# Twenty-eight dummy products behind a chunk's state products, and the first r·k moved behind the table of k

## The chip, the cores and the metric

The kernel runs on one core of one Trainium2 chip. The metric is device time in microseconds, as the median of several executions. Profiles are of one execution each, with the times of all instructions counted from the first.

## What is computed

Three stages follow each other on batches of 4 x 768 tokens with 8 heads of 48 channels (384 channels in all). The dense products of the MLP are each done as three products of a high and a low part.

```
# 1. linear attention with a decaying state, per batch and head
for t in range(S):
    y[t]  = r[t] @ (state + outer(u * k[t], v[t]))
    state = w[:, None] * state + outer(k[t], v[t])
# 2. a gated MLP with a mix over tokens
h = gelu(x @ w_in);  u, v = split(h)
v_n = layernorm(v) * g_ln
v_s = einsum('ts,bsd->btd', w_sg, v_n) + b_sg[None, :, None]
x2  = x + (u * v_s) @ w_out
# 3. a gated projection with a causal convolution of 5 taps
out = (sigmoid(conv5(x2)) * (x2 @ w_val)) @ w_out2
```

## The kernel before, in words

**Attention.** The 768 tokens of a batch are six chunks of 128, so there are 24 chunks, numbered 0 to 23 ("chunk 8" is the ninth). A chunk's loads are `rp`, `kp` and `v`. TensorE transposes r and the scaled k (`att_T`, line 652), which are multiplied by tables of powers of w on the way out of PSUM (`tabR`, `tabK`; made in `tables`, lines 321 to 357). Then come scores (`S_products`, line 678; from chunk 6 on `S_blocks`, line 749), the state's products k^T v (`KV_products`, line 705; from chunk 6 on `KV_blocks`, line 783) and the outputs (lines 840 to 875). GpSimd makes r·k (`dv`), which for chunk 0 stands in `tables` as `dv0`. The results go through HBM into the rows `xf`.

**MLP.** For each batch: projections V0 to V5 (the half v of h, 128 tokens each, `mlp_V`) and U00 to U13 (the half u, 384 tokens by 128 channels, `mlp_U`), then the mix over tokens (`mlp_SG`, S00 to S13, with `wsg`, the parts of w_sg, and `vh`, the normalised v), `mlp_O1`, `mlp_VAL` and `mlp_O2`. Each product of the three parts is a call of `three` (lines 1091 to 1093). w_sg is scaled by a power of two that its own sum of squares sets: ScalarE squares it (line 444), TensorE adds (line 465), VectorE makes the scale (lines 473 to 479), ScalarE and VectorE make the parts (`psg`, line 494 and a helper), and SP turns them with transposing DMAs (line 497).

**What sets the order.** All of the program's order is fixed when it is built. `go` is a planner: it has streams of TensorE's work (attention and MLP), and chains of steps on ScalarE (A), VectorE (V), GpSimd (P) and SP's queue (Q), with assumed costs, and puts out instructions in the order of planned times. On the chip each engine goes through its list in order and waits on semaphores. The first lines of the lists are written by hand (`consts`, `load_w`, `tables`).

**Dummy products.** `fill(n)` issues n products of a matrix of ones with itself, 128 columns each, into the PSUM tile `warm` (`self.pf`), whose result nobody reads. The planner calls it in the gaps that it sees for TensorE in the first 30 us of its plan; `S_products` and `att_Y` call it by hand for chunk 0.

**PSUM.** Its eight banks are three pools: one bank for `pw`, NPA = 4 for attention (`pa`) and 7 - NPA = 3 for the MLP (`pm`). `warm` is the first tile of `pm`. A bank goes to another tile when the last instruction on the tile that has it has been issued, and that tile's first product then waits until it is done with; the planner itself counts three tokens for `pm`.

```
"pa": NPA, "pm": 7 - NPA
self.pf = self.pm.tile([P, 512], F32, tag="pm", name="warm")
nc.tensor.matmul(self.pf[:, 0:P], self.onesb, self.onesb, start=True, stop=True)
```

**Places that matter below.** The small vectors g_ln and b_sg are loaded by `load_small`, whose place in SP's queue is set by `AFTER_SM`. At the end of the last batch `mlp_O2` puts `LAST_FILL` dummies behind the last products.

Of the kernel before, what the change touches and what calls it, by code (L numbers as in the profile page):

```python
# [32 lines left out]
class Kern:  # L33
# [145 lines left out]
    def go(self, streams, choose):  # L179
# [3 lines left out]
        while True:  # L183
# [9 lines left out]
            if n is None:  # L193
# [5 lines left out]
                t = min(soon)  # L199
                n = int((t - self.now) * (FILL0 if self.now < 14000 else FILL) / (112 if self.now < 4000 else 56)) if self.now < FILL_END else 0  # L200
                if n:
                    self.fill(FILLS.get(self.n_fill, n))
                    self.n_fill += 1
# [116 lines left out]
    def tables(self):  # L320

        nc = self.nc
        M = Q
        self.tabR = self.const([HR, NP, P], F32, "tabR")
        self.tabK = self.const([HR, NP, P], F32, "tabK")
        self.W = self.const([HR, NP], F32, "W")
        q = self.Rst(F32)[:HR, 0:NP * (Q + 1)].rearrange("d (p n) -> d p n", p=NP)
        wq, rw = (self.const([HR, NP], F32, n) for n in ("wq", "rw"))
        t = self.Rst(F32)[:HR]
        z, y, e = (t[:, n * NP * M:(n + 1) * NP * M].rearrange("d (p n) -> d p n", n=M) for n in range(3))  # L330
        nc.gpsimd.memset(z, 0.0)
        nc.gpsimd.memset(q[:, :, 0:1], 1.0)


        nc.vector.tensor_scalar(wq, self.wP, W_LEAST, W_MOST, ALU.max, ALU.min)

        def scan(src, dst):
            for p in range(NP):
                nc.vector.tensor_tensor_scan(dst[:, p], src[:, p:p + 1].to_broadcast([HR, M]), z[:, p], 1.0, ALU.mult, ALU.add)

        scan(wq, q[:, :, 1:])
        nc.scalar.copy(self.tabR[:, :, 0:M], q[:, :, 0:M])
        nc.gpsimd.tensor_mul(self.tabR[:, :, M:], q[:, :, 0:M], q[:, :, M:].to_broadcast([HR, NP, M]))
        nc.vector.reciprocal(rw, wq)
        scan(rw, y)


        nc.vector.scalar_tensor_tensor(e, q[:, :, 1:], -1.0, y, ALU.mult, ALU.mult)
        nc.vector.scalar_tensor_tensor(self.tabK[:, :, 0:M], e, 2.0, y, ALU.add, ALU.mult)

        def second(e):
            e.tensor_mul(self.tabK[:, :, M:], self.tabK[:, :, 0:M], self.tabK[:, :, M - 1:M].to_broadcast([HR, NP, M]))
            e.tensor_mul(self.W, q[:, :, M:].rearrange("d p o -> d (p o)"), q[:, :, M:].rearrange("d p o -> d (p o)"))

        self.dv0(nc.gpsimd)
        second(nc.gpsimd)
        self.mark("tabS0", T_S)

# [313 lines left out]
    def S_products(self, i):  # L672
        nc = self.nc
        rT, kT = self.kr[i]
        pA, pB = self.ps_a(), self.ps_a()
        for p in range(NP):
            for ps, r0 in ((pA, 0), (pB, 64)):
                nc.tensor.matmul(ps[:, p * P:(p + 1) * P], kT[r0:r0 + D, p, :], rT[r0:r0 + D, p, :], start=True, stop=True)
        self.mark(("S", i))
        if not i:  # L680
            self.fill(12)
        mb = self.mask.unsqueeze(1).to_broadcast([P, NP, P])
        parts = self.scores[i] = []
        for n, ps in enumerate((pA, pB)):

            def masked(e, ps=ps):
                t = self.wp.tile([P, NP, P], F32, tag="sc", name=self.nm("sc"), bufs=2)
                e.tensor_mul(t, ps.rearrange("s (p t) -> s p t", t=P), mb)
                parts.append(t)

            self.chain(("sc", i, n), ("V", 602.0, masked, ["sc"], ["pa"]), after=[("Y", i - 1)] if i else [], prio=pr(i))
# [80 lines left out]
    def KV_blocks(self, i, X):  # L772

        nc = self.nc
        c = i % NCH
        kS, vt = self.kS[i], self.vt[i]
        halves = range(2 if c != NCH - 1 else 1)
        c0 = NP * Q
        for p in range(NP):
            for j in range(2):  # L780
                for h in halves:
                    ts = slice(h * Q, (h + 1) * Q)
                    nc.tensor.matmul(X[h][64 * j:64 * j + 64, c0 + p * D:c0 + (p + 1) * D], kS[ts, 2 * p + j, :], vt[ts, 2 * p + j, :], start=True, stop=True)  # L783
        self.mark(("KV", i))
        for h in halves:
            n = 2 * i + h
            kv = X[h][:HR, c0:c0 + NP * D].rearrange("d (p e) -> d p e", e=D)
            given = []
            fresh = not c and not h

            def add(e, h=h, n=n, kv=kv, given=given, fresh=fresh):
                told, tnew = self.T2[n % 3], self.T2[(n + 1) % 3][:, :, 0:D]
                e.tensor_copy(tnew, kv) if fresh else e.tensor_add(tnew, kv, told[:, :, 0:D])  # L793
                self.X_read(i, h, given)

            def decay(e, n=n):
                tnew = self.T2[(n + 1) % 3][:, :, 0:D]
                if e is nc.scalar:
                    for p in range(NP):
                        e.activation(tnew[:, p], tnew[:, p], AF.Copy, scale=self.W[:, p:p + 1])  # L800
                else:
                    e.tensor_mul(tnew, tnew, self.W.unsqueeze(2).to_broadcast([HR, NP, D]))

            self.chain(
                ("kv", i, h), ("V", 290.0, add, [], given), *([("AP", {"A": 1120.0, "P": 560.0}, decay)] if h else []),
                after=[("Y", i - 1)] + (["T2"] if i == QUAD else []) + ([("kv", i, 0)] if h else [("kv", i - 1, 1)] if c else []), prio=pr(i),
            )
# [444 lines left out]
    def mlp_O2(self, b, half, q, dst=None):  # L1252
# [13 lines left out]
        if b == B - 1 and half:  # L1266
            if q == 2:
                pz = self.ps_m()
                for _ in range(LAST_FILL):
                    nc.tensor.matmul(pz[:, 0:P], self.onesb, self.onesb, start=True, stop=True)  # L1270
# [182 lines left out]
def pr(i):  # L1453

    return 0 if i < NCH else PR_A if i >= 2 * NCH or i < FROM_B else PR_B
# [6 lines left out]
FROM_B, PR_B = 9, 2.5  # L1462
RAW, PR_RAW = 13, 2.5
QUAD, PAST_NS = 6, 520
AFTER_SG, AFTER_SM, AFTER_CW = 6, 6, 9
WA, WM = 4, 4
NW = 3
NR, NS, NA, NX, NY, NL, NV, NPA = 12, 10, 3, 3, 2, 3, 2, 4
# [9 lines left out]
HOLD_G, HOLD_S, TURN = 200.0, 0.0, 1500.0  # L1478
HOLD = {"gelu": HOLD_G, "sigmoid": HOLD_S}
FILL, FILL0 = 0.6, 0.8  # L1480
FILL_END = 30000.0
FIRST = "V0 U00 V1 U01 V2 U02 V3 U03 V4 V5"
LAST = "U10 S00 U11 S01 U12 S02 U13 S03 O00 O01 O02 S10 S11 A00 A01 A02 S12 S13 P00 O10 P01 O11 P02 O12 A10 A11 A12 P10 P11 P12"
# [1 line left out]
BODY = "U10 S00 U11 S01 U12 S02 U13 S03 O00 O01 O02 S10 S11 A00 A01 A02 S12 S13 P00 O10 P01 O11 P02 O12 v0 A10 u00 A11 v1 A12 v2 u01 u02 v3 u03 P10 v4 P11 P12 v5"  # L1485
END = "U10 S00 U11 S01 U12 S02 U13 S03 O00 O01 S10 S11 O02 S12 S13 A00 A01 A02 O10 O11 O12 P00 P01 A10 A11 A12 P02 P10 P11 P12"
LATER = ['a', 'a', 'a', 'a', 'a', 'a']
FILLS = {}
LAST_FILL = 5
W_LEAST, W_MOST = 0.75, 1.0  # L1490
N_OK = HR * NP

# [41 lines left out]
```

## Time and profile before

| | us |
|---|---|
| median of 3 runs | 434.7 (433.62 to 434.74) |
| the profiled execution's own time | 432.49 |
| its span, first to last instruction | 430.7 |
| TensorE products busy | 411.3 (96%) |
| VectorE busy | 346.6 (80%) |
| ScalarE busy | 207.1 (48%) |
| GpSimd busy | 208.9 (49%) |
| mean granted TensorE clock | 0.996 |

A row of the profile's order of time has a start and a duration in us, the engine, the line, the operation, the tiles as out<-in, a count if rows were joined, and in brackets the idle time of the engine just before, with what ended it. The ends of products are modelled: of products that follow each other the distance of the starts is what one costs. [...]

### The profile page before, as it was taken

The page shows a single profiled execution, that of the slowest core. Times are in us where ns is not written, and L with a number is a line of the kernel's source. Part 1 is how long each engine was busy: PE and PEld are TensorE (multiplying, and loading weights), DVE is VectorE, ACT ScalarE, POOL GpSimd, SP SyncE. Part 2 cuts the span into 40 slices and gives each one's busy share as a digit, 9 for nine tenths or more (in the row PEclk, how much of TensorE's full clock was granted, in tenths as well). Part 3 has the DMA queues.
Part 4 walks back from the last instruction along what each step waited for, and adds up shares of the span by engine and source line. Part 5 has one row for each costly group of instructions (what it writes and reads, how often), then busy time and mean ns, then how long its engine had stood idle before and what let it go on. Part 6 is the DMA issues. An engine that isn't in the chain of part 4 may idle for free. (4 is left out here: it accounts for less than half of the span.)

```text
span 430.7 us, 11575 instructions
## 1 busy us (share of the span) xinstructions
PE 411.3 (96%) x4616; PEld 346.9 (81%) x4616; DVE 346.6 (80%) x740; ACT 207.1 (48%) x439; POOL 208.9 (49%) x243
## 2 busy tenths in 40 slices
PE   7988998889999999999999999899999999999996
PEld 7776787857787999877887999777878989776896
DVE  6887899987899788788989799777786696649992
ACT  2546667754464486534253486532132763104152
POOL 6776976466267657673597757652110322100000
PEclk9999999989999999999999999999999999999999
DMA  6998997699646716764558541632002001000012
GB/s 164 204 237 190 256 274 188 129 198 204 171 87 133 195 47 152 175 163 107 126 124 211 148 113 37 176 84 55 20 2 91 18 2 55 2 0 2 0 38 79
DMA packets 128955, 50.15 MB, mean 116 GB/s; under 512 B 90752, under 2 KB 126720, under 8 KB 128896
## 3 DMA queue, kind: packets, MB, share of 16 engines
q1 hardware_dynamic: 128464, 48.76, 46.5%
q8 instruction: 38, 0.62, 0.6%
q10 hardware_dynamic: 432, 0.59, 0.4%
q14 instruction: 21, 0.17, 0.1%
HBM read 37.54 MB, written 9.44 MB: 109 GB/s over the span
## 5 line engine op out<-in xcount | busy, mean ns | idle before, releaser
L1091 PE MATMUL pm<-wsg,vh 128*128 128x384 f16 x192 | 63.6, 331 | 0.6 <-DVE S L1242 0.6
L1093 PE MATMUL pm<-wsg,vh 128*128 128x384 f16 x192 | 63.2, 329 | 0.0
L1092 PE MATMUL pm<-wsg,vh 128*128 128x384 f16 x192 | 63.1, 329 | 0.0
L1212 DVE SCALAR_TENSOR_TENSOR words<-xf,cw,words 128x384 f32<-128x384 f32 x72 | 44.3, 615 | 3.3 <-ACT words L1210 2.3
L1424 POOL TENSOR_TENSOR R<-S,R 128x384 fp32r<-128x384 f32 x16 | 16.0, 1008 | 56.3 <-ACT R L1450 51.2
L1424 POOL TENSOR_TENSOR ks<-kp,tabS 128x384 f32<-128x384 f32 x24 | 24.3, 1012 | 26.8 <-PE pa L783 13.4
L1091 PE MATMUL pm<-R,win 128*128 128x384 f32 x96 | 34.1, 355 | 1.0 <-ACT S L1148 1.0
L1091 PE MATMUL pm<-R,wout 128*128 128x384 f32 x96 | 33.2, 346 | 0.0
L1092 PE MATMUL pm<-R,wout 128*128 128x384 f32 x96 | 32.3, 336 | 0.1
L1093 PE MATMUL pm<-R,win 128*128 128x384 f32 x96 | 32.3, 337 | 0.0
L1092 PE MATMUL pm<-R,win 128*128 128x384 f32 x96 | 32.2, 335 | 0.0
L1093 PE MATMUL pm<-R,wout 128*128 128x384 f32 x96 | 32.2, 335 | 0.0
L1178 DVE SCALAR_TENSOR_TENSOR S<-pm,gs,b_bc 128x384 f32<-128x384 f32 x32 | 19.6, 614 | 15.2 <-PE pm L1093 13.9
L1450 ACT CAST R<-S 128x384 fp32r<-128x384 f32 x33 | 16.7, 511 | 29.3 <-DVE S L1424 14.4
L1091 PEld LDWEIGHTS <-vh 128*128 128x128 f16 x192 | 19.0, 99 | 14.5 <-issue 3.5
L1093 PE MATMUL pm<-win,R 128*128 128x512 f32 x72 | 28.7, 398 | 1.7 <-DVE R L988 1.7
L1424 POOL TENSOR_TENSOR R<-xf,R 128x384 fp32r<-128x384 f32 x12 | 12.1, 1012 | 37.0 <-ACT R L1450 21.3
L1091 PE MATMUL pm<-win,R 128*128 128x512 f32 x72 | 28.7, 398 | 0.5 <-ACT R L984 0.5
L1093 PEld LDWEIGHTS <-vh 128*128 128x128 f16 x192 | 18.9, 98 | 12.6 <-issue 0.3
L1092 PEld LDWEIGHTS <-vh 128*128 128x128 f16 x192 | 19.0, 99 | 12.0 <-issue 1.5
L1092 PE MATMUL pm<-win,R 128*128 128x512 f32 x72 | 28.4, 395 | 0.0
L1424 POOL TENSOR_TENSOR rs<-rs,exps 128x1 f32<-128x1 f32 x24 | 14.3, 597 | 29.0 <-DVE rs L1114 20.1
(196 smaller groups left out, 1226.6 us busy)
## 6 DMA issues: line engine op xcount, KB each, us to landing
rp<-in_r_dram SPq DMA_DIRECT2D x24, 192.0 KB, 3.6
kp<-in_k_dram SPq DMA_DIRECT2D x24, 192.0 KB, 4.0
v<-in_v_dram SPq DMA_DIRECT2D x24, 192.0 KB, 3.8
xd<-yT SPq DMA_DIRECT2D x48, 96.0 KB, 2.2
xf<-xd SPq DMA_DIRECT2D x24, 192.0 KB, 2.7
raw<-in_r_dram SPq DMA_DIRECT2D x43, 96.0 KB, 2.6
raw<-in_k_dram SPq DMA_DIRECT2D x43, 96.0 KB, 2.5
out_dram<-S SPq DMA_DIRECT2D x21, 192.0 KB, 1.9
```

What stands on the lines that cost most here:

```text
L1091: nc.tensor.matmul(ps, lh, rh, start=m == 0, stop=False)
L1092: nc.tensor.matmul(ps, lh, rl, start=False, stop=False)
L1093: nc.tensor.matmul(ps, ll, rh, start=False, stop=m == total - 1)
L1178: ("V", 529.0, lambda e: e.scalar_tensor_tensor(t, pg[:, :TH], self.gs[:, d:d + 1], self.b_bc[:, ts], ALU.mult, ALU.add), [], ["pm"]),
L1212: eng.scalar_tensor_tensor(t, row[:, j:j + TH], self.cw[:, e, j:j + 1], t, ALU.mult, ALU.add)
L1424: self.made.append(call(*a, **kw))
L1450: return "AV", {"A": 413.0, "V": 269.0}, lambda e: e.copy(dst, src()) if hasattr(e, "copy") else e.tensor_copy(dst, src()), [], list(give)
```

## The change

Four things move. (1) Behind the state products of chunk 8 stand 28 dummies. (2) In `tables` the product r·k of chunk 0 moves from ahead of `tabK`'s second half to behind it, on GpSimd. (3) The numbers of dummies change: behind the first scores 22 for 12, in the planner's gaps ahead of them 14 for 29 and 9 for 14 (the later gaps keep their counts), and 16 for 5 at the very end. (4) `load_small` follows chunk 5's loads, not chunk 6's.

```diff
         def second(e):
             e.tensor_mul(self.tabK[:, :, M:], ...)
+            self.dv0(e)
             e.tensor_mul(self.W, ...)
-        self.dv0(nc.gpsimd)
         second(nc.gpsimd)
...
         if not i:
-            self.fill(12)
+            self.fill(22)
...
                     nc.tensor.matmul(X[h][64 * j:64 * j + 64, ...], kS[ts, 2 * p + j, :], vt[ts, 2 * p + j, :], start=True, stop=True)
+        self.fill(KV_FILL.get(i, 0))
         self.mark(("KV", i))
...
-AFTER_SG, AFTER_SM, AFTER_CW = 6, 6, 9
+AFTER_SG, AFTER_SM, AFTER_CW = 6, 5, 9
...
+KV_FILL = {8:28}
...
-FILLS = {}
-LAST_FILL = 5
+FILLS = {7:8,8:2,9:3,10:1,13:3}
+LAST_FILL = 16
```

**TensorE, the first projections.** The rows are the end of U01 and the beginning of V2 (third of the v projections), with the semaphores that a product waits for. Before:

```order
L1091 MATMUL pm_1025<-R_607,win_96 128x384
L1092 MATMUL pm_1025<-R_607,win_96 128x384
L1093 MATMUL pm_1025<-R_607,win_97 128x384
L1091 MATMUL pm_1043<-win_96,R_605 128x512
L1092 MATMUL pm_1043<-win_97,R_605 128x512
```

The same place of the changed program:

```order
L1092 MATMUL pm_1015<-R_597,win_96 128x384
L1093 MATMUL pm_1015<-R_597,win_96 128x384
L1094 MATMUL pm_1015<-R_597,win_97 128x384
L1092 MATMUL pm_1033<-win_96,R_595 128x512 [waits Activation_49]
L1093 MATMUL pm_1033<-win_97,R_595 128x512
```

No product has moved, but V2's first product now waits for ScalarE: `warm` is in use until chunk 8, so the projections ahead of it go round two banks, and V2 takes the one that U00 had.

**GpSimd, the tables.** The rows follow `tabR`'s second half. Before:

```order
L343 TENSOR_TENSOR tabR<-Rst_156 112x4x64
L589 TENSOR_TENSOR dv_136<-rp_123,kp_126 128x8x48
L352 TENSOR_TENSOR tabK<-tabK 112x4x64
L353 TENSOR_TENSOR W<-Rst_156 112x4
L1424 TENSOR_TENSOR dv_136<-dv_136,u_bc 128x8x48
```

Of the changed program:

```order
L343 TENSOR_TENSOR tabR<-Rst_156 112x4x64
L352 TENSOR_TENSOR tabK<-tabK 112x4x64
L589 TENSOR_TENSOR dv_136<-rp_123,kp_126 128x8x48
L354 TENSOR_TENSOR W<-Rst_156 112x4
L1425 TENSOR_TENSOR dv_136<-dv_136,u_bc 128x8x48
```

The product r·k has gone past one instruction, and stands ahead of the small product W.

**SP, the small loads.** Before:

```order
L910 DMA xf_519<-xd_59 128x3x128
L530 DMA rp_124<-in_r_dram 128x8x48
L530 DMA kp_127<-in_k_dram 128x8x48
L316 DMA g<-in_moe_g_ln_dram 128x4x1
L318 DMA b_bc<-in_moe_b_sg_dram 128x768
```

Of the changed program:

```order
L911 DMA xf_509<-xd_59 128x3x128
L316 DMA g<-in_moe_g_ln_dram 128x4x1
L318 DMA b_bc<-in_moe_b_sg_dram 128x768
L530 DMA rp_124<-in_r_dram 128x8x48
L530 DMA kp_127<-in_k_dram 128x8x48
```

The two small loads have gone past the loads of r and k of chunk 7.

## Rows read from the trace of the kernel before

**Rows 1.** Window of 2 us: busy us (instructions) of each engine, granted clock, DMA.

```profile
90.00:92.00 2.00, 2.00 (x8) 0.97 (x8) 1.69 (x2) 2.00 (x3) 1.51 (x2) 0.50 1.26 262
```

**Rows 2.** Order of time, TensorE and VectorE from chunk 8 to the mix over tokens.

```profile
88.07 0.43 DVE L757 COPY_PREDICATED dv<-mask,pa 128x256 f32<-128x256 int16 x1
...
88.60 0.62 PE L652 MATMUL pa<-ident,rp 128*112 128x128 f32 x4 [2.09 <-issue]
...
89.61 0.52 PE L1091 MATMUL pm<-wsg,vh 128*128 128x384 f16 x1
...
92.53 0.45 PE L1091 MATMUL pm<-wsg,vh 128*128 128x384 f16 x1
...
93.14 0.33 PE L1091 MATMUL pm<-wsg,vh 128*128 128x384 f16 x1
...
93.31 0.33 PE L1092 MATMUL pm<-wsg,vh 128*128 128x384 f16 x1
```

**Rows 3.** Order of time, the projections U00, V2 and U02 and ScalarE's gelu.

```profile
54.89 0.44 PE L1091 MATMUL pm<-R,win 128*128 128x384 f32 x1
...
58.12 0.39 PE L1091 MATMUL pm<-win,R 128*128 128x512 f32 x1
...
60.36 0.85 ACT L1148 ACTIVATE S<-pm 128x384 f32<-128x384 f32 x2
...
60.88 0.44 PE L1091 MATMUL pm<-R,win 128*128 128x384 f32 x1 [0.51 <-ACT S L1148]
```

**Rows 4.** Order of time, chunk 7's state products and VectorE's reading of them.

```profile
71.03 0.63 PE L783 MATMUL pa<-v,ks 64*64 64x48 f32 x32
...
72.51 0.35 DVE L793 TENSOR_TENSOR T<-pa,T 112x192 f32<-112x192 f32 x1
```

**Rows 5.** Order of time, projections U12 and U13, ScalarE, and chunk 8's scores.

```profile
77.66 2.59 ACT L494 ACTIVATE psg<-st,sb 128x768 f16<-128x768 f32 x3 [0.49 <-DVE sb L478]
...
78.45 0.33 PE L1091 MATMUL pm<-R,win 128*128 128x384 f32 x1
...
80.15 1.23 ACT L1148 ACTIVATE S<-pm 128x384 f32<-128x384 f32 x3
...
80.67 0.45 PE L1091 MATMUL pm<-R,win 128*128 128x384 f32 x1 [0.49 <-ACT S L1148]
...
85.36 0.69 PE L749 MATMUL pa<-rT,kT 48*64 48x64 f32 x32 [0.85 <-DVE vh L1424]
```

**Rows 6.** Order of time, TensorE, the next mix over tokens.

```profile
129.09 0.32 PE L1091 MATMUL pm<-wsg,vh 128*128 128x384 f16 x1 [0.60 <-DVE S L1242]
```

**Rows 7.** Line 339, the scans of both tables: count, ns min/median/max, start us.

```profile
L339 DVE TENSOR_TENSOR_SCAN Rst<-wq,Rst x4: 266/268/295, 4.3 to 4.8; 112x64 f32<-112x64 f32 x4
L339 DVE TENSOR_TENSOR_SCAN Rst<-rw,Rst x4: 259/464/1047, 5.2 to 6.9; 112x64 f32<-112x64 f32 x4
```

**Rows 8.** Order of time, the head.

```profile
5.86 1.01 POOL L589 TENSOR_TENSOR dv<-rp,kp 128x384 f32<-128x384 f32 x1
...
8.86 0.60 PE L366 MATMUL pa<-ident,tabK 112*128 112x112 f32 x4 [1.55 <-POOL tabK L352]
...
10.45 0.51 ACT L379 ACTIVATE words<-Rst 128x384 f32<-128x384 f32 x1 [0.47 <-DMA Rst<-in_moe_w_in_dram]
...
11.64 1.00 POOL L1424 TENSOR_TENSOR ks<-kp,tabS 128x384 f32<-128x384 f32 x1 [1.28 <-DVE words L1424]
...
11.85 0.84 PE L222 MATMUL warm<-onesb 128*128 128x128 bf16 x12
```

**Rows 9.** Order of time, SP's small loads, and GpSimd's r·k of chunk 7.

```profile
37.39 3.05 SPq L316 DMA_DIRECT2D g<-in_moe_g_ln_dram  x1
...
40.49 0.50 SPq L318 DMA_DIRECT2D b_bc<-in_moe_b_sg_dram  x1
...
48.52 1.02 POOL L1424 TENSOR_TENSOR kp<-rp,kp 128x384 f32<-128x384 f32 x1
```

**Rows 10.** Order of time, TensorE, the dummies at the very end.

```profile
426.46 0.45 PE L1270 MATMUL pm<-onesb 128*128 128x128 bf16 x5
```

## The prediction, made before the run

> **What bounds the kernel now.** I read the page first: TensorE's products cover 96% of the span, so I looked for the stretches where it waits, and for those where it is slow. [...] From 93.14 on its products follow each other every 0.17 us; the ten between 89.61 and 92.53, counted along the order of time, take nine steps in 2.92 us [rows 2]. The projections before that are not TensorE's alone: U02 idled 0.51 us and U13 0.49 us for ScalarE's gelu, chunk 8's scores 0.85 us for other engines [rows 3, 5]. So up to 90 us TensorE, ScalarE and VectorE wait for each other in turn. Later TensorE waits little, but where it does, as for 0.60 us at 129.09, it is for VectorE [rows 6]. What a stretch before 90 us loses is passed on; what TensorE alone gains near 90 us may be lost at the next wait for VectorE.
>
> **The 28 dummies, their own time.** Twelve dummies of the head take 0.84 us, so one costs at most 0.07 us [rows 8], and 28 at most 1.96 us. They stand where TensorE idles 2.09 us [rows 2]: cost 0. The cover is the wait for VectorE's copy; were it gone, the cost would be up to 1.96 us.
>
> [...]
>
> **What they cost elsewhere: a PSUM bank.** The dummies write `warm`, the first tile of the MLP's pool of three banks. Before, its last use lay ahead of the first projection. Now it lies behind chunk 8, so V0 to U13 share two banks, as the new wait of V2's first product shows. Step by step:
>
> - V2 takes U00's bank. Before, it started at 58.12, in a third bank. U00's gelu is the first of the pair at 60.36, and U02, which waited for just that, started at 60.88 [rows 3]. So V2 starts at 60.88, 2.76 us late. U02's idle 0.51 us is then gone, and it starts 60.88 - 58.12 - 0.51 = 2.25 us late. I carry 2.2.
> - Behind U02 TensorE has no wait until chunk 7's state products at 71.03, so these end at 73.9, not 71.66. VectorE read them at 72.51 [rows 4], so VectorE is late by 1.4 (73.9 - 72.51) to 2.2 us. The scale of w_sg and then `psg` on ScalarE hang on it: 77.66 becomes 79.1 to 79.9 [rows 5]. I take 1.6 us, nearer the lower end, since `psg` itself follows an idle 0.49 us of ScalarE that may take up some.
> - ScalarE's gelu of U10 stands behind `psg` in its queue: 80.15 becomes 81.75. U12 needs the bank of U10, so it starts at the end of that gelu, 81.75 + 1.23/3 = 82.2, not at 78.45 [rows 5]. U13, nine steps of 0.17 behind, starts at 83.7, not 80.67: 3.0 us late.
> - The idle 0.85 us ahead of chunk 8's scores swallows a part [rows 5]: 2.2 us late. The state products, the dummies, VectorE's copy and the start of the mix follow, so it starts at 89.61 + 2.2 = 91.8.
>
> **What is left at the end.** TensorE makes good 1.4 of 2.2 us. VectorE, which is not faster, stays late by what it was: between 1.4 (its lateness at chunk 7) and 2.2 (at chunk 8). At 129.09 TensorE waits for VectorE, so from there the lateness of VectorE counts. I take 1.9 us, nearer the later end.
>
> [...]
>
> **The head.** The third scan of `tabK` takes 1.047 us, where the same scan for `tabR` takes 0.268 [rows 7], and it stands beside GpSimd's r·k, 5.86 to 6.87 [rows 8]. With r·k behind the table, `tabK` can be 0.78 us earlier, its transposes start at 8.1 and not 8.86, and the first scores come earlier too. But behind them ScalarE waits for w_in's DMA until 10.45, VectorE for that, and GpSimd's scaled k at 11.64 for VectorE [rows 8]; none of it depends on `tabK`. So the gain is 0 (bounds: 0 and 0.8). The moved r·k runs from about 8.1 to 9.1, and GpSimd's idle 1.28 us ahead of the scaled k takes it up. Of the dummies, 22 behind the scores take at most 22 x 0.07 = 1.54 us. With the scores ending 0.78 us earlier, at 11.1, they are done by 12.6, ahead of the scaled k at 12.64: cost 0, or up to 0.7 us if the scores don't move.
>
> **The small loads.** The load of r and k of chunk 7 is issued 3.05 + 0.50 = 3.55 us later, and SP is back in step behind it. Its first reader on GpSimd starts at 48.52 [rows 9], so a load that goes out at 40 has over 8 us: cost 0, and at most the same 3.55 us if that reader waited. The 16 dummies at the end, at most 0.09 us each, are done by 427.9 [rows 10], inside the span of 430.7: cost 0.
>
> **Sum.** 0 + 1.9 + 0 = +1.9 us on the profiled execution's own 432.49, so 434.4. The median of the runs is 434.7, 2.2 us above that execution, so the forecast is **436.6**. About 0.3% (1.3 us) is what a measurement of this kernel can tell from no change.
>
> **Rivals.**
>
> *The clock falls in the new gaps* (slower by more). TensorE now idles 2.76 us ahead of V2 and, by the steps above, some 2 us ahead of U12. The clock fell behind a gap of 2.09 us [rows 1, 2], so it may fall there. It costs about what the old fall cost, 1.4 us, and that delays the gelu that others wait for. The time is 436.6 + 1.4 = 438.0. Against it: TensorE works at full clock on both sides of these gaps, and the idle 1.55 us ahead of `tabK`'s transposes passed without a fall [rows 8]. [...]
>
> *Faster: the lateness never reaches chunk 8.* The mechanism is that chunk 8's scores are set by other engines, as their idle 0.85 us suggests. It decides at TensorE being under 0.85 us late there. Then only the clock counts: 434.7 - 1.4 = 433.3. For it: the wait named in the row. Against: U12 must wait for a gelu that stands behind `psg`, which alone makes U13 over 1.5 us late even with `psg` in time.
>
> *Nothing left at the end.* The clock's 1.4 us meets a lateness that VectorE's waits have worn down to its lower bound, 1.4 us: 434.7 - 1.4 + 1.4 = 434.7, or up to 436.0 where TensorE keeps only part of the gain.
>
> *The change does not hold the clock*: the fall has other causes than this gap. Then 1.4 us of TensorE's gain is missing; by the sum VectorE sets the end anyway, with 2.2 us late at most plus what is lost in the mix: 437 to 438, in one case with the first rival.
>
> **How the numbers follow.** The forecast, with its own range of 436.1 to 437.3 (VectorE late by 1.4 to 2.6), has 0.42. The first and last rival together have 0.18, faster 0.18, nothing left 0.22. So slower by over 0.3% has 0.42 + 0.18 = 0.60, within 0.3% 0.22, faster 0.18. The range reaches down to the faster case, 433.2, and up to the clock's case with 0.6 us for the bounds of the head, 438.6.
>
> **What would show it.** Right: V2 starts right behind U00's gelu, over 2 us idle ahead of it; U12 starts behind U10's gelu; the mix over tokens starts at 91 to 92.5 with products every 0.17 us; the clock is 1.00 from 86 to 96; at 129 the same product starts 1.4 to 2.6 us later. In the head the third scan is near 0.27 us, and the scaled k is still at 11.6. Wrong: V2 at 58, or the mix at 89.6 or before. A granted clock of 0.50 between 58 and 66 would be the first rival.

## The result, and the profile after

The changed kernel takes 438.28 us (median of 6 runs, 437.18 to 441.07), the kernel before 433.89 us in the same comparison (6 runs). The ratio is 1.0105, with a 95% interval of 1.0075 to 1.0134: the change makes the kernel 1% slower. The profiled execution took 440.0 us, with a span of 438.2 us; that of before took 432.49 and 430.7. The two stand at opposite ends of their kernels' executions (the change's second highest of six; before's below all but one of its six), so of the 7.5 us between these two spans only 4.4 us are the difference of the medians.

The order of time shows the steps of the prediction (start, duration, engine, line, operation; in brackets the idle time before and what ended it). The row at 61.78 is V2, the row at 84.69 is U12, those at 95.77 and 97.24 are the first and the tenth product of the mix:

```profile
55.88 0.44 PE L1092 MATMUL pm<-R,win 128*128 128x384 f32 x1
...
61.26 0.85 ACT L1149 ACTIVATE S<-pm 128x384 f32<-128x384 f32 x2
61.78 0.80 PE L1092 MATMUL pm<-win,R 128*128 128x512 f32 x1 [2.50 <-ACT S L1149]
...
65.57 0.60 ACT L1130 ACTIVATE A<-pm 128x512 f32<-128x512 f32 x1 [3.04 <-PE pm L1094]
66.20 0.69 DVE L1131 BATCH_NORM_STATS2 bst<-A 128x6 f32<-128x512 f32 x1 [3.81 <-ACT A L1130]
...
81.68 2.59 ACT L494 ACTIVATE psg<-st,sb 128x768 f16<-128x768 f32 x3 [0.49 <-DVE sb L478]
...
84.69 0.44 PE L1092 MATMUL pm<-R,win 128*128 128x384 f32 x1 [1.79 <-ACT S L1149]
...
91.44 0.67 PE L749 MATMUL pa<-rT,kT 48*64 48x64 f32 x32
...
92.50 1.74 PE L222 MATMUL warm<-onesb 128*128 128x128 bf16 x28
94.88 0.62 PE L652 MATMUL pa<-ident,rp 128*112 128x128 f32 x4 [0.65 <-issue]
95.77 0.33 PE L1092 MATMUL pm<-wsg,vh 128*128 128x384 f16 x1
...
97.24 0.33 PE L1092 MATMUL pm<-wsg,vh 128*128 128x384 f16 x1
...
134.84 0.32 PE L1092 MATMUL pm<-wsg,vh 128*128 128x384 f16 x1 [0.55 <-DVE S L1243]
...
431.82 1.07 PE L1271 MATMUL pm<-onesb 128*128 128x128 bf16 x16
```

Against the rows of before, the same instruction starts this much later: U00 0.99 us (55.88 against 54.89), V2 3.66 (against 58.12), both in [rows 3]; `psg` 4.02 and U12 6.24 and chunk 8's scores 6.08 [rows 5]; the mix 6.16, its tenth product 4.71 [rows 2]; the product that waits for VectorE 5.75 [rows 6]; the dummies of the end 5.36 [rows 10]. Between the mix's first and tenth product TensorE makes good 1.45 us: the clock is held there, at 1.00 from 94 to 98 us, where before it was 0.50 in 90 to 92 [rows 1]. The span itself is 7.5 us longer, so 2.1 us come behind the last product.

The windows of 2 us (busy us of each engine, granted clock as a share of full speed, DMA) show where the clock fell instead:

```profile
62.00:64.00 2.00, 2.00 (x5) 1.60 (x6) 0.39 (x1) 0.53 (x2) 1.47 (x2) 0.50 0.91 271
...
86.00:88.00 2.00, 2.00 (x8) 2.00 (x7) 1.94 (x5) 0.49 (x1) 0.81 (x2) 0.50 1.12 91
...
92.00:94.00 2.00, 2.00 (x67) 1.95 (x60) 1.41 (x4) 1.50 (x4) 1.03 (x2) 1.00 0.60 119
```

Ahead of both falls TensorE idled for a gelu, 2.50 us before V2 and 1.79 us before U12: one long idle ahead of each fall. In this execution the clock was also at 0.50 in 45 to 47 us, behind an idle 1.17 us that ended at 42.45. There the change was still 0.58 us ahead of before (43.03); with the fall, U00 is 0.99 us late. The row of the same place before shows no fall behind an idle 1.07 us, nor does the change with 5 dummies at the end behind 1.18 us, so this idle alone does not make the fall.

The head (the first row is the third scan of `tabK`), and the output's DMA at the end (the last row is of all outputs from 415 us on, issue to landing; the 4.0 is the last output's):

```profile
5.95 0.26 DVE L339 TENSOR_TENSOR_SCAN Rst<-rw,Rst 112x64 f32<-112x64 f32 x1
...
8.06 0.61 PE L366 MATMUL pa<-ident,tabK 112*128 112x112 f32 x4 [0.24 <-POOL tabK L352]
...
10.82 0.52 ACT L379 ACTIVATE words<-Rst 128x384 f32<-128x384 f32 x1 [1.64 <-DMA Rst<-in_moe_w_in_dram]
...
12.02 0.99 POOL L1425 TENSOR_TENSOR ks<-kp,tabS 128x384 f32<-128x384 f32 x1 [1.43 <-DVE words L1425]
...
432.52 0.34 ACTq L1272 DMA_DIRECT2D out_dram<-S  x1
...
DMA to landing us min/median/max: 1.8/2.0/4.0
```

The third scan took 1.05 us before and now takes 0.26, and `tabK` is 0.80 us earlier. Nothing comes of it, because ScalarE waits for w_in's DMA [rows 8]. The last issue ends at 432.86, 5.3 us ahead of the end of the span. Before, the rows at the same places read:

```profile
5.96 1.05 DVE L339 TENSOR_TENSOR_SCAN Rst<-rw,Rst 112x64 f32<-112x64 f32 x1
...
427.16 0.34 ACTq L1271 DMA_DIRECT2D out_dram<-S  x1
...
DMA to landing us min/median/max: 1.9/1.9/2.8
```

There it is 3.2 us (430.7 less 427.50); the 2.8 is the output before the last, and the last one's landing is in no row.

### The profile page after: what moved, and what is told of

Its sections match the earlier page's. It is cut to its first block, busy times and chain, and to the rows that moved or that the text cites. A ratio compares the mean times of both kernels' runs of the same rounds, so it can differ in the third digit from the quotient of the medians.

```text
span 438.2 us, 11636 instructions
## 1 busy us (share of the span) xinstructions
PE 417.9 (95%) x4645; PEld 353.4 (81%) x4645; DVE 345.1 (79%) x740; ACT 206.8 (47%) x439; POOL 208.7 (48%) x243
## 5 line engine op out<-in xcount | busy, mean ns | idle before, releaser
L1092 PE MATMUL pm<-R,win 128*128 128x384 f32 x96 | 34.8, 363 | 1.8 <-ACT S L1149 1.8
L1094 PE MATMUL pm<-R,win 128*128 128x384 f32 x96 | 32.9, 343 | 0.0
L1093 PE MATMUL pm<-R,win 128*128 128x384 f32 x96 | 32.9, 343 | 0.0
L1092 PE MATMUL pm<-win,R 128*128 128x512 f32 x72 | 29.5, 410 | 2.9 <-ACT S L1149 2.5
L1094 PE MATMUL pm<-win,R 128*128 128x512 f32 x72 | 29.2, 405 | 1.8 <-DVE R L989 1.8
L1092 PEld LDWEIGHTS <-vh 128*128 128x128 f16 x192 | 18.7, 98 | 14.2 <-issue 3.0
L1093 PE MATMUL pm<-win,R 128*128 128x512 f32 x72 | 28.9, 401 | 0.0
L1094 PEld LDWEIGHTS <-vh 128*128 128x128 f16 x192 | 18.8, 98 | 12.4
L1149 ACT ACTIVATE S<-pm 128x384 f32<-128x384 f32 x32 | 15.4, 486 | 27.4 <-PE pm L1094 27.4
```

Of the source, the lines that this page charges most:

```text
L1092: nc.tensor.matmul(ps, lh, rh, start=m == 0, stop=False)
L1093: nc.tensor.matmul(ps, lh, rl, start=False, stop=False)
L1094: nc.tensor.matmul(ps, ll, rh, start=False, stop=m == total - 1)
L1149: self.chain(("u", b, half, f), ("A", ("gelu", 371.0), lambda e: e.activation(t, pu[:, :TH], AF.Gelu_apprx_tanh), [], ["pm"]))
```

## The experiments

All times are medians; each kernel ran beside the kernel before on one chip, and the ratio is to that. The kernel before itself took 433.9 to 435.2 us in the five comparisons, so an expected time can be missed by a microsecond for that reason alone; the ratios decide. In the traces of all runs but the one with xf ahead of a transpose, the engines do the same work in the same order as in the kernel that the run starts from, apart from the dummies.

| kernel | us | before, same comparison | ratio (95%) |
|---|---|---|---|
| the change | 438.28 | 433.89 | 1.0105 (1.0075 to 1.0134) |
| 28 dummies in their own bank | 435.85 | 434.32 | 1.0024 (0.9990 to 1.0057) |
| before + 28 dummies on `warm` | 436.65 | 434.32 | 1.0045 (1.0010 to 1.0081) |
| before + 1 dummy on `warm` | 437.64 | 434.32 | 1.0084 (1.0056 to 1.0113) |
| the change without the 28 | 435.00 | 434.32 | 1.0016 (0.9987 to 1.0045) |
| before + 16 dummies at the end | 437.21 | 435.22 | 1.0050 (1.0021 to 1.0079) |
| the change, 5 at the end | 439.49 | 435.22 | 1.0084 (1.0053 to 1.0116) |
| before + 28 in their own bank | 435.24 | 435.22 | 1.0010 (0.9981 to 1.0039) |
| the change, own bank, 5 at the end | 434.90 | 435.22 | 0.9992 (0.9968 to 1.0016) |
| the change, its new gaps filled | 438.80 | 434.52 | 1.0089 (1.0055 to 1.0123) |
| before + own bank + dummies ahead of `okb` | 434.39 | 434.52 | 0.9995 (0.9970 to 1.0020) |
| the same, xf ahead of a transpose | 447.89 | 434.52 | 1.0286 (1.0245 to 1.0327) |
| before + own bank + `okb`, none at the end | 434.03 | 435.12 | 0.9977 (0.9950 to 1.0003) |

**The bank: dummies in a tile of their own.**

```diff
-        self.fill(KV_FILL.get(i, 0))
+        n_kv = KV_FILL.get(i, 0)
+        if n_kv:
+            own = self.ps_m()
+            for _ in range(n_kv):
+                nc.tensor.matmul(own[:, 0:P], self.onesb, self.onesb, start=True, stop=True)
```

Expected:

> The changed kernel, but the 28 dummies write a pm tile of their own, taken at chunk 8, so warm is released after the head again. Theory (the bank): V2 starts again at 58 to 59 us with no wait for a gelu, U12 with none, the new falls of the clock at 61 and 85 us are gone, the mix over tokens starts at 89.5 to 90.5 us at full clock; the time is 432.5 to 434.5, 4 to 5.5 us under the changed kernel. Rival (the dummies' own time, or the other edits): nothing but the tile has changed, so the time stays at 437 to 439.

Measured: 435.85 us, a ratio of 1.0024, between the two expected ranges: 1.35 us above the top of the first. Against the change's 1.0105 this is 0.8% or 3.5 us less, and the two intervals do not meet. Its order of time has the old starts again:

```profile
58.12 0.39 PE L1096 MATMUL pm<-win,R 128*128 128x512 f32 x1
...
60.78 0.45 PE L1096 MATMUL pm<-R,win 128*128 128x384 f32 x1 [0.42 <-ACT S L1153]
...
89.36 0.33 PE L1096 MATMUL pm<-wsg,vh 128*128 128x384 f16 x1
...
100.10 5.32 SPq L497 DMA_TRANSPOSE wsg<-psg  x3
...
106.15 0.38 SPq L956 DMA_DIRECT2D xf<-xd  x1
...
110.00 0.36 DVE L1429 CAST R<-xf 128x384 fp32r<-128x384 f32 x1 [2.02 <-DMA xf<-xd]
...
112.75 0.32 PE L1096 MATMUL pm<-wsg,vh 128*128 128x384 f16 x1 [1.55 <-DVE xf L1203]
```

V2 is at 58.12, to the hundredth where it was [rows 3], and the mix's products are 0.25 us (first) to 1.5 us earlier. So V2's wait is the bank's. But then VectorE waits 2.02 us for a load of xf that stands on SP behind three transposing DMAs, and TensorE waits 1.55 us for VectorE: in this profile the clock's gain is gone 15 us after it was made. These three DMAs took 5.32 us here and 4.00 us in before's profile, and the product at 112.75 stands at 111.71 before, so a part of that wait is this execution's. What is still missing led to the end of the kernel, below.

**The parts of the change, one by one.** Before, with 28 dummies and with a single one on `warm`, and the change without the 28:

```diff
+        self.fill(KV_FILL.get(i, 0))
         self.mark(("KV", i))
...
+KV_FILL = {8:28}
```

```diff
+        self.fill(KV_FILL.get(i, 0))
...
+KV_FILL = {8:1}
```

```diff
-KV_FILL = {8:28}
+KV_FILL = {}
```

Expected, in this order:

> The kernel before with the 28 dummies on warm behind chunk 8 and nothing else. Theory (the bank): the whole loss is here, 437 to 439; V2 and U12 wait for gelus, 2 to 3 us idle each. Rival (the head and load edits make the loss): 432.5 to 434.5, as before or a little faster for the held clock.

> The kernel before with a single dummy on warm behind chunk 8: warm is held just as long, but neither 28 products' time nor their hold on the clock is there. Theory (the bank): V2 and U12 wait as with 28, and the clock falls behind chunk 8 as in the kernel before; 438 to 440.5, up to 1.4 us over the run with 28. Rival (the 28 products' own time): one product costs at most 0.07 us, so 433.5 to 434.5, as before.

> The changed kernel without the 28 dummies: the head, the dummy counts, the small loads and the end alone. Theory (the bank): nothing is left of the loss, 433 to 435, with the fall of the clock behind chunk 8 as before. Rival (these edits make the loss): 437 to 439.

Measured: 436.65, 437.64 and 435.00 us. The single dummy is the clearest: one product, 0.84% slower, if 0.36 us under its expected range. V2 idles 2.49 us, U12 1.80 us, and the clock falls behind chunk 8 as before (0.56 in 94 to 96 us):

```profile
59.98 0.73 PE L1092 MATMUL pm<-win,R 128*128 128x512 f32 x1 [2.49 <-ACT S L1149]
...
83.07 0.44 PE L1092 MATMUL pm<-R,win 128*128 128x384 f32 x1 [1.80 <-ACT S L1149]
...
90.88 0.23 PE L222 MATMUL warm<-onesb 128*128 128x128 bf16 x1
93.26 0.62 PE L652 MATMUL pa<-ident,rp 128*112 128x128 f32 x4 [2.15 <-issue]
94.16 0.46 PE L1092 MATMUL pm<-wsg,vh 128*128 128x384 f16 x1
94.40 0.53 PE L1093 MATMUL pm<-wsg,vh 128*128 128x384 f16 x1
94.72 0.53 PE L1094 MATMUL pm<-wsg,vh 128*128 128x384 f16 x1
```

The mix's products stand 0.32 us apart there, as at the clock of 0.50 before [rows 1, 2], and 0.17 with 28. So what costs is how long `warm` lives, not the 28 products' own time, and what they hold is the clock. The run with 28 was expected to have the whole loss, 437 to 439, and is 0.35 us under that; by its ratio it has 2.0 us of the loss. If that is not noise (the two intervals just overlap), something else in the change costs too, although the run without the 28 has only 0.7 us over before, with an interval that takes in 0. In the profile of that run the span ends 5.2 us behind the last issue's end, as in the change; in the two with 5 dummies at the end it is 3.2 us.

**The end.** Before with 16 dummies behind the last products, and the change with 5:

```diff
-LAST_FILL = 5
+LAST_FILL = 16
```

> The kernel before with 16 instead of 5 dummies at the very end, nothing else. Theory (the end): a load of instructions on TensorE's queue then falls into the last output's transfer; one sixteenth of that output lands about 1.1 us later, and the span ends 5.2 us after the start of its last issue has ended, not 3.2: 2.0 us more, 436 to 436.8. Rival (the dummies lie inside the span, as predicted): 434.3, as before.

> The changed kernel with 5 dummies at the end, as before. Theory (the end): 2.0 us less than the changed kernel, 436 to 436.8, all of the rest of the loss being the PSUM bank's. Rival (the end costs nothing): 438.3.

Measured: 437.21 us, 2.0 us over before, as expected of the end (0.4 us above the range in microseconds); and 439.49 us, which is 0.9 us less than the change by the ratios, not 2.0. The second is not what the theory said in time, though the two intervals overlap so far that neither 0 nor 2.0 us is excluded. Its rows do say it: the span ends 3.2 us behind the last issue's end (434.96 to 438.2). The execution profiled had the clock at 0.50 in 61 to 63, 85 to 87 and 283 to 285 us; the change's has three falls too (45, 62 and 86 us), so they do not explain why the time fell by less. What the 11 dummies do shows in the DMA packets. First the last issue of before with 16 dummies, and two windows of its DMA, 430.50 to 431.75 and 431.75 to 433.50 (queue: packets, MB, share of 16 engines):

```profile
429.80 0.34 ACTq L1271 DMA_DIRECT2D out_dram<-S  x1
...
q10 hardware_dynamic: 135, 0.18, 40.3%
q8 instruction: 1, 0.02, 5.3%
...
q10 hardware_dynamic: 9, 0.01, 3.1%
...
DMA to landing us min/median/max: 1.9/1.9/3.9
```

Then the kernel before, in the window of its last output, 428.00 to 429.50, and in that of 425.50 to 426.50:

```profile
q10 hardware_dynamic: 144, 0.20, 36.3%
...
q8 instruction: 1, 0.02, 7.3%
```

An output has 144 packets. Before, the load of instructions falls into 425.5 to 426.5, ahead of the last issue at 427.16, and the last output lands in one piece. With 16 dummies it falls into the last output's transfer; 135 packets land by 431.75 and 9, a sixteenth, behind them. 9 packets are one engine's share of 144, so it looks as if they stood behind the instructions on one of the 16 engines. The rows do not name the engine, but all five profiles with 16 dummies bear it out: in each, 135 packets have begun by 1.51 us behind the start of the last issue, and the first of the other 9 begins when the load of instructions ends, to 0.02 us (in the run shown the load goes from 1.61 to 2.68 us, and the first late packet begins at 2.67). In all eight profiles with 5 dummies the span ends 3.2 us behind the last issue's end; with 16 it is 5.2 to 5.3 us in four, where the load ends 2.57 to 2.68 us behind the start of the issue, and 4.4 in one (the filled gaps), where it ends at 1.88.

**The held clock alone, and both causes taken out.** The kernel before with the 28 in their own tile; the change with that and 5 dummies at the end:

> The kernel before with 28 dummies behind chunk 8 in a pm tile of their own: the held clock alone, without the bank. Theory (the gain is lost): the mix's first ten products take 1.5 us, not 2.9, but at 111.7 us TensorE waits for VectorE, which waits for a load of xf behind SP's transposing DMAs, so the time is 433.7 to 434.8. Rival (the gain comes through): 432.6 to 433.2.

> The changed kernel with the 28 dummies in a tile of their own and 5 dummies at the end. Theory (bank and end are the whole loss): 433.3 to 434.5, no slower than before. Rival (the head's or the loads' edits cost something too): 435 or more.

Measured: 435.24 us, 1.0010, and 434.90 us, 0.9992, each 0.4 us above its first range. Holding the clock behind chunk 8 is worth nothing that can be measured: the first profile has its mix's products up to 1.7 us earlier, and at 111.78 TensorE waits 0.56 us for VectorE, level with before's 111.71. That the gain goes just there is argued from profiles: the kernel before with 16 dummies at the end, whose clock fell at 89 to 92 us, waits 2.00 us at the same product. And with bank and end put right the rest of the change, the head's order, its dummies and the small loads, costs and gives nothing that can be measured (by the interval 1.4 us less to 0.7 us more): the predicted zeros hold.

**The stall without the falls of the clock.** The change with dummies in its new gaps, in `mlp_V` ahead of V2 and in `mlp_U` ahead of U12:

```diff
             if c == 0:
+                self.fill(V_FILL.get((b, i), 0))
...
             if c == 0:
+                self.fill(U_FILL.get((b, half, f), 0))
                 pu = self.ps_m()
...
+V_FILL = {(0, 2): 36}
+U_FILL = {(0, 1, 2): 26}
```

> The changed kernel, warm held as there, with 36 dummies ahead of V2 and 26 ahead of U12, in the two gaps that the missing bank opens. [...] Rival (the clock is the whole loss): 433.5 to 434.5 plus the end's 2.0, so 435.5 to 436.5, with the mix starting at 90. Rival (the clock costs nothing): 438.3.

Measured: 438.80 us, above both rivals' times, and above the 436 to 437.5 expected if stall and clock add up and the falls' part, about 1.5 us, goes. Its profile (of the fastest of the seven executions, 436.83 us) shows V2 and U12 right behind the gelus and no fall:

```profile
57.90 2.19 PE L222 MATMUL warm<-onesb 128*128 128x128 bf16 x36
60.57 0.50 PE L1092 MATMUL pm<-win,R 128*128 128x512 f32 x1 [0.49 <-ACT S L1151]
...
79.05 2.59 ACT L494 ACTIVATE psg<-st,sb 128x768 f16<-128x768 f32 x3 [0.49 <-DVE sb L478]
...
80.12 1.63 PE L222 MATMUL warm<-onesb 128*128 128x128 bf16 x26
82.07 0.44 PE L1092 MATMUL pm<-R,win 128*128 128x384 f32 x1 [0.32 <-ACT S L1151]
...
87.25 0.67 PE L749 MATMUL pa<-rT,kT 48*64 48x64 f32 x32
...
91.58 0.33 PE L1092 MATMUL pm<-wsg,vh 128*128 128x384 f16 x1
...
130.90 0.32 PE L1092 MATMUL pm<-wsg,vh 128*128 128x384 f16 x1 [0.45 <-DVE S L1245]
```

The clock is 1.00 in every window from 40 us to the last product, and the mix starts at 91.58, not 95.77. By these two profiles 2.0 us of the mix's lateness are the bank's wait, and 4.2 us are the falls and what hangs on them. But one is the fastest of its kernel's executions and the other the second slowest, the executions' median (438.80, near the second rival's 438.3) is no lower than the change's own, and the intervals overlap, so what the falls cost in time is not shown. The other six executions took 438.7 to 440.6 us; what they lost is in no profile here.

The change's own six executions speak for a price. Profiles with 16 dummies at the end have a mean clock of 0.999 without a fall, 0.994 with one and 0.987 with three. The change took 437.18, 437.77 and 437.90 us at a mean clock of 0.995, 438.66 at 0.991, and 440.00 and 441.07 at 0.987 and 0.986: about 1.5 us more for each further fall (an estimate from these six; that the falls are the cause of it is not shown). The three with about one fall are still 3.3 to 4.0 us over before.

**Trying for a version that beats both.** The clock also fell behind TensorE's wait for `okb` (276 to 283 us) in several profiles, as to 0.50 in 278 to 280 us in that of the change with own bank and 5 at the end; before's profile, where that wait is 1.69 us and ends at 275.00, has 1.00 from 274 to 284. 24 dummies ahead of that product, on top of the own bank; then also the load of xf ahead of the last transposing DMA; and, instead, no dummies at the end:

```diff
+        hold = self.ps_a()
+        for _ in range(24):
+            nc.tensor.matmul(hold[:, 0:P], self.onesb, self.onesb, start=True, stop=True)
         pt = self.ps_a()
```

```diff
...
+        if i >= LATE_SG:
+            self.chain(("psg", i), *steps[:3], prio=prio, after=first)
+            self.chain(("w_sg", i // 3), steps[3], prio=prio, after=[("psg", i), ("y", 1, 2)])
...
+LATE_SG = 5
```

```diff
-LAST_FILL = 5
+LAST_FILL = 0
```

> The kernel before with 28 dummies in a tile of their own behind chunk 8 and 24 dummies ahead of the product of okb, where TensorE waits 1.7 us for VectorE and the clock fell behind it in several profiles. Theory: no fall is left in the span, the mean clock is 1.00 in every run; 433 to 434.5, 0 to 1.3 us under the kernel before. Rival: the time follows VectorE and the loads, 434.3 to 435.2, as before.

> As the run with dummies ahead of okb, and on SP the load of xf of chunk 8 stands ahead of the last of w_sg's transposing DMAs, and no longer behind it. Theory (the held clock's gain was lost at the wait for this load): the load is issued some 1 us earlier, VectorE no longer waits 1 to 2 us for it, TensorE does not wait at 111.7 us, and the time is 432 to 433.5, about 1.4 us under the kernel before. Rival (the next wait takes the gain): 433.5 to 435.

> As the run with dummies ahead of okb, without any dummies at the very end. Theory (the end): with 5 dummies the load on TensorE's queue lies 1 to 1.5 us ahead of the last output's issue and delays only the output before it; with none it lies there or earlier, so the last output lands 1.9 to 2.8 us after its issue and the span ends 2.3 to 3.2 us after that issue has ended; 433.5 to 434.5. Rival (the end costs what the dummies' number says): no change of the 3.2 us, 434.4.

Measured: 434.39, 447.89 and 434.03 us. The first keeps the clock: its window of 278 to 280, and under it that of the change with own bank and 5 at the end, without those dummies:

```profile
278.00:280.00 2.00, 2.00 (x11) 1.70 (x10) 0.37 (x2) 1.67 (x3) 1.74 (x2) 1.00 0.86 232
```

```profile
278.00:280.00 2.00, 2.00 (x8) 2.00 (x8) 1.26 (x3) 1.29 (x2) 1.71 (x3) 0.50 0.90 219
```

In eight of its twelve executions the mean clock is 0.998 or more, in four 0.996; the own bank alone has seven of twelve, and the third run, which has the 24 dummies too, all twelve. So the falls are not gone with them, and that they are rarer is not sure. 434.39 lies in both expected ranges; by the ratio (0.9995) it is the time of before, the rival. The second failed: the planner put the whole order behind that place differently, and the load was issued at 105.10, no earlier than 105.03 before; TensorE then idled 9.37 us for VectorE at 142.97. It says nothing on the load. The third is the lowest of all, 1.1 us under before, with an interval that just reaches 1. Its last output lands 2.3 us after its issue, as expected:

```profile
DMA to landing us min/median/max: 2.3/2.3/2.3
```

But the span ends 3.6 us behind that issue's end, later than with 5 dummies. The load of instructions did move forward: it begins 2.1 us ahead of the last issue, where it is 0.9 to 1.3 us with 5, and the output two before the last now lands 3.7 us after its issue. Why the span gains nothing by it is open. No version here is shown to beat the kernel before.

## Why the prediction was right, and where it was not

The direction and the range (433.2 to 438.6) were right; 438.28 is 1.7 us above the forecast of 436.6 and outside that case's own range (436.1 to 437.3, whose upper bound of 2.6 us late is worked out nowhere). Against before in the same comparison the change costs 4.4 us, where 1.9 were forecast: before's median there was 433.89, not the 434.7 that the forecast started from. That the range held is in part luck: its top stood on the first rival and on 0.6 us for the head, and the head cost nothing that shows, while the end, counted as 0, cost up to 2.0 us.

Of the signs that it named, V2 and U12 behind their gelus and the third scan (0.26 us) came. In the change's profile the mix (95.77), the clock (0.50 in 86 to 88), the product of 129 (5.75 us late) and the scaled k (12.02) did not, and 0.50 in 62 to 64 us was the sign of the first rival.

- *The 28 dummies cost nothing.* Right: they take 1.74 us, and 0.65 us of the gap is left behind them.
- *The clock is worth 1.4 us on TensorE.* Right. The 1.4 us are what the mix's nine steps at 0.50 took, 2.92 us, less 9 x 0.17 = 1.53, the later steps' pace [rows 1, 2]; the dummies were to keep the clock at 1.00 there. In the change's profile they did, and the nine steps took 1.47 us, 1.45 less. The single dummy, with the fall back in its place, shows that it was that gap.
- *The bank.* The mechanism was right, and with the clock held so were its sizes on TensorE; in time, with the falls that it brings, the bank cost 3.5 to 4.0 us by three of four pairs of runs and not 1.9. V2 starts behind U00's gelu; against U00 it is 2.67 us later than before (3.66 - 0.99), where 2.76 was worked out. With the clock held, the run with filled gaps meets the chain: `psg` at 79.05 (79.3 forecast), U12 at 82.07 (82.2), chunk 8's scores at 87.25, 1.89 us late (2.2), the mix at 91.58 (91.8), and 1.81 us late where TensorE waits for VectorE (1.9). One part was reasoned wrongly: VectorE's lateness was taken from chunk 7's state products, with up to 0.8 us of slack and no wait of TensorE ahead of them (before's trace has one, 0.31 us at 70.52). In the change's profile it comes earlier, from V2's own statistics, for which VectorE idles 3.81 us, and all of it goes on to `psg` (4.02 us).
- *The step that failed: the 16 dummies at the end "are done by 427.9 [rows 10], inside the span of 430.7: cost 0".* The dummies of the end are done in time, and yet 11 more of them lengthen the span by 2.0 us, through a load of instructions that meets the last output. In time that is 2.0 us in the run made for it, by the medians, and 0.7 to 1.4 us by the other pairs (the change without the 28 against before; own bank with 16 and with 5; the change with 16 and with 5). Only the dummies' own time had been bounded.
- *The first rival, the clock falls in the new gaps*, came true beside the forecast: all four profiles that hold `warm` and leave the gaps empty show a fall at V2, and three of them one at U12 too. Its price of 1.4 us is near the 1.5 us a fall of the change's own executions, but the run with filled gaps does not confirm it.
- *The faster case* has nothing left: the held clock alone gives 1.0010. By the profiles the gain is lost as the prediction feared, only sooner, at 111.7 us and not at 129, behind a load of xf that VectorE needs. (Against this case it put U13 "over 1.5 us late"; by its own numbers that is 1.4: 80.15 + 0.41 + 1.53 less 80.67.)
- *Head and small loads: 0.* Right. The third scan went from 1.05 to 0.26 us with r·k out of its way; the second, beside `tabR`'s product on GpSimd before and after, stays at 0.64. The scaled k starts at 12.02, 0.38 us later, with the w_in DMA that it hangs on.
- *The price of the bank, by pairs of runs.* Going from three banks to two costs 3.6 us with a single dummy, and giving the bank back gains 3.5 us (16 dummies at the end) to 4.0 us (5). Only 28 dummies against 28 in their own bank, on the kernel before, say less, 1.5 us.

What stays open: how much of the loss is the bank's wait alone and how much the falls of the clock that it brings. The parts, 2.0 us (28 on `warm`) and 0.7 us (the rest), sum to less than the 4.6 us of the whole by the ratios; each interval is some 1.3 to 1.6 us wide to either side, so the 1.9 us between them may be noise.

## What to carry to other kernels

Here a single dummy product that kept its PSUM tile alive made V2 wait 2.49 us for a gelu and the kernel 0.84% slower: ask of each dummy where its tile was last used before, and whose bank that takes. Give dummies that stand late a tile taken there. Instructions at the very end were not free for fitting into the wait for the last output, 2.0 us for 16 dummies in place of 5: look at the DMA queues in the last microseconds too. And a clock held for 1.4 us of TensorE's time was worth nothing that could be measured here (a ratio of 1.0010), so look first for the next wait for another engine.

## What the runs showed that was not expected

- A load of instructions (one packet, 0.02 MB) during the last output's transfer: 135 of 144 packets land on time, 9 up to 2 us late, beginning as the load ends, and the span ends 2.0 us later.
- With the same list on SP, the three transposing DMAs of w_sg that stand ahead of that load of xf keep it for 3.96 us (before with 16 dummies at the end), 4.00 us (before) or 5.42 us (before with 28 on `warm`). In before with 16 dummies at the end, whose program is that of before up to the last product, TensorE waited 2.00 us at 113.50, where before's profile shows none. A single profile's difference of 2 us is not a cause here.
- The number of falls shows in a kernel's own executions, though not in all kernels: before with 28 dummies on `warm` took 434.35 to 436.25 us in its six executions with a mean clock of 0.996 or more, 437.04 to 439.08 in the five at 0.992 and 440.57 in the one at 0.988. In others, as the one with filled gaps, the clock was full and the time high all the same.
